# A gated feed-forward block after windowed attention: gate and up of two token chunks as a 2x2 block product with seven products

## The chip, the cores and the metric

One core of one Trainium2 chip. The metric is the time of one execution on the device in microseconds; three runs of the kernel before had a median of 698.26 us (697.82 to 700.38).

## What is computed

A pre-norm transformer block on x of 2048 tokens by 448: attention with 16 heads of 28 and a causal window of 256, then a gated feed-forward part of width 1792. All of it is in float32.

```python
h = x + attention(layernorm(x)) @ wo
y = layernorm(h)
g = y @ w_gate            # 448 x 1792
u = y @ w_up              # 448 x 1792
out = h + (gelu_tanh(g) * u) @ w_down   # 1792 x 448
```

## The kernel before, in words

**Numbers.** TensorE works in a float32 format with a shortened mantissa (fp32r). So every operand is split into a high part (`to_hi`, a copy on ScalarE) and a low part (`to_lo`, a subtraction on VectorE or GpSimd), and each product is the sum of three: high by high, low by high, high by low. A depth of 448 is three blocks of 128 rows and one of 64; the half blocks of two of the three products are laid on each other, so that a product of depth 448 takes 11 matmuls (`TERMS`, `NP`) where 10.5 would do.

**Order.** A planner (`Lists`) receives every operation with engine, cost, key, tokens read and written, and PSUM bank, simulates the engines, refines the keys in `ROUNDS` rounds from `SEED`, and emits the instructions in that order. Each engine then runs its own queue in order and waits on semaphores. The numbers in `op(...)` are the planner's costs.

**Attention** fills the first part. The second layer norm (`layer_norms`, kind "ln2", and `turn`) writes a normalized tile of 128 tokens to DRAM transposed and reads it back into `xT`, split in high and low part; this goes on beside attention's end and the first products.

**Feed-forward.** `product(n, i, c, ...)` works on a tile of 128 of the 1792 hidden columns (i) and a chunk of 512 of the 2048 tokens (c): 14 tiles by 4 chunks, 56 products, in four groups of tiles (`GROUPS`). The first four (`PAIRED = 4`) are whole: 11 matmuls of 128 rows and 512 columns for gate and 11 for up. From the fifth on every matmul is cut into two of 64 rows that run at the same time in the two halves of the array, one for gate and one for up, then with the halves exchanged (`pair`, `phase`): 21 pairs instead of 22 whole matmuls. Then ScalarE makes the gelu (L1125), VectorE the product with up (L1127), ScalarE and VectorE the high and low part (L487, L490), and the down product follows: 12 pairs of 448 columns into four banks that add up over a group, and VectorE adds them to `hres` (L1158). Between phases ScalarE reads one element of a bank (`seen`, L1068), which orders the two halves. Weights: 14 records of 1472 columns are loaded by SyncE's queue into one of three raw buffers (`weight_load`) and split by ScalarE and VectorE (the first three with GpSimd, `weight_splits`) into seven places (`RECS`).

All matmuls pass through the helper `mul` (L484), all high parts through L487, all low parts through L490: these lines are told apart by their tiles.

Of the kernel before, what the change touches and what calls it, by code (L numbers as in the profile page):

```python
# [18 lines left out]
NG = 4  # L19
# [6 lines left out]
GROUPS = [3, 4, 4, 3]  # L26
REC = 2944
NB = NG * CS
# [12 lines left out]
LEAD = 110  # L41
# [3 lines left out]
SWAP = -60  # L45
# [3 lines left out]
AHEAD = 7  # L49
BEHIND = 5  # L50
# [3 lines left out]
PAIRED = 4  # L54
MOVED = 0
SPANS = {"pp", "proj", "raw", "xT", "h", "rqf", "rkf", "vm", "rec0", "rec1", "rec2"}
# [13 lines left out]
ROUNDS = 220  # L70
SEED = 33
# [295 lines left out]
def block_kernel(ctx: ExitStack, tc, x, wqk_in, wv_in, wo_in, ffn_in, out):  # L367
# [16 lines left out]
    xT = pool.tile([128, 7, S], F32R, name="xT")  # L384
    rq_m = pool.tile([128, 4096], F32R, name="rq")
    rk_m = pool.tile([128, 6144], F32R, name="rk")
# [7 lines left out]
    last_hi = pool.tile([128, 128], F32R, name="lasthi")  # L394
    mhl = [pool.tile([128, 96], F32R, name=f"mhl{i}") for i in range(3)]
# [10 lines left out]
    back = pool.tile([128, 40], F32, name="back")  # L406

# [12 lines left out]
    ohl = lp.tile([128, 2, 2, 512], F32R, name="ohl")  # L420
    rec = []

    def open_rec():
        fst.close()
        p = ctx.enter_context(tc.tile_pool(name="fp", bufs=1))
        rec.extend(p.tile([128, REC], F32R, name=f"rec{i}") for i in range(2))
        rec.append(p.tile([128, S], F32R, name="xh"))


    rq = [rq_m[:, 2048 * u:2048 * u + 2048].rearrange("p (j t) -> p j t", j=4) for u in range(2)]  # L430
# [141 lines left out]
    def turn(t, key):  # L572
        c = slice(t * 128, (t + 1) * 128)
        d = xn_d[t]
        xb, at = (v_m[:, REC:REC + D], span("vm", REC, D)) if t > 7 and t % 2 else (xn[1], ("xn", 1))
        op("dve", 0.56, 0.65, key, lambda: nc.vector.transpose(xb, xn[0]), [("xn", 0)], [at], port=True)
        for a in range(4):
            dst = d.rearrange("(b i) t -> i b t", i=32)[:, :, 32 * a:32 * a + 32]
            src = xb[32 * a:32 * a + 32].rearrange("i (b t) -> i b t", t=32)
            dma(key, 150, lambda dst=dst, src=src: nc.sync.dma_start(dst, src), [at], [("xnd", t, a)])  # L580
        put = [("xnd", t, a) for a in range(4)]
# [13 lines left out]
        op("act", 0.7, 0.82, key + 0.2, hi, [("xt3", t)], [XT(t), "lasthi"])  # L595
        op("dve", 0.75, 0.82, key + 0.2, lo, [XT(t), "lasthi"], [XT(t)], port=True)
# [357 lines left out]
    def flat(m, name, o):  # L954
# [5 lines left out]
    RECS = [(lambda o=o, m=m, name=name: flat(m, name, o), flat(m, name, o)[1], need) for m, name, o, need in (  # L960
        (proj_m, "proj", 0, None), (proj_m, "proj", REC, None), (rq_m, "rqf", 0, "ringfree"),
        (rk_m, "rkf", 0, "ringfree"), (rk_m, "rkf", REC, "ringfree"))] + \
# [47 lines left out]
    def feed_forward():  # L1010
# [32 lines left out]
        for m in range(PAIRED, n):  # L1043
            for ph in phase[m]:
                order += [ph, todo.pop(0)]
# [270 lines left out]
```

## Time and profile before

| | us |
|---|---|
| median of three runs | 698.26 |
| profiled execution | 698.08 |
| its span, first to last instruction | 696.4 |
| TensorE busy | 687.8 |
| VectorE busy | 396.9 |
| ScalarE busy | 362.4 |
| GpSimd busy | 158.7 |

A busy time is the sum of what the engine's records cover. Matmuls overlap in the pipe, so the length of one record (0.376 us for a matmul of 512 columns) is longer than the distance to the next; what a matmul costs is read from the distance between starts. The same holds for VectorE. "PEld" is the load of weights, which runs beside the matmuls.

### The profile page before, as it was taken

What the parts mean: (1) busy time and instruction counts of PE and PEld (TensorE: products, weight loads), DVE (VectorE), ACT (ScalarE), POOL (GpSimd) and SP (SyncE); (2) the same over time, 40 slices, a digit from 0 to 9 for tenths busy, and PEclk for the clock granted to TensorE, in tenths of its full rate; (3) what the DMA queues carried; (4) which work ended last, traced back from release to release, by engine and by line L of the source; (5) the groups of instructions that cost most, each with busy time, mean ns of one, the idle gap of its engine ahead of it and who ended that gap; (6) DMA issues with size and microseconds to landing.
All of it is one profiled execution on the core that took longest, in us unless ns stands there. A gap on an engine that the chain in (4) does not pass through costs nothing.

```text
span 696.4 us, 15402 instructions
## 1 busy us (share of the span) xinstructions
PE 687.8 (99%) x5897; PEld 604.7 (87%) x5897; DVE 396.9 (57%) x1057; ACT 362.4 (52%) x930; POOL 158.7 (23%) x253
## 2 busy tenths in 40 slices
PE   8999999999999999999999999999999999999997
PEld 8998888888888887778899999999999999999996
DVE  7987877876687978877764232245232244333224
ACT  7658767776767888896653222234222234222221
POOL 5604434344454653753100000000000000000000
PEclk9999999999999999999999999999999999999999
DMA  8888647475556688524663000012100000001012
GB/s 297 262 282 243 210 150 229 141 213 164 176 168 197 160 247 226 157 55 95 146 188 131 1 2 2 1 44 88 45 1 2 1 1 2 1 1 55 10 45 106
DMA packets 83138, 79.12 MB, mean 114 GB/s; under 512 B 34104, under 2 KB 72952, under 8 KB 83064
## 3 DMA queue, kind: packets, MB, share of 16 engines
q1 hardware_dynamic: 83064, 78.14, 37.4%
q8 instruction: 46, 0.75, 0.4%
q14 instruction: 28, 0.23, 0.1%
HBM read 48.23 MB, written 29.36 MB: 111 GB/s over the span
## 4 chain that ended last, share of the span: by engine, by line
PE 91%; ACT 3%; DVE 3%; issue 1%; POOL 1%; DMA 0%; DVEq 0%; ACTq 0%
PE bank L484 85%; PE bank L894 5%; PE bank L542 1%; ACT pp L864 1%; ACT xn L537 1%; ACT xT L487 1%; DVE bnst L519 1%; ACT rq L487 0%; DVE xT L490 0%; DVE mt L792 0%; DVE hres L941 0%; POOL bnve L511 0%; PE bank L819 0%; DMA hres<-in_x_dram 0%; ACT proj L487 0%
## 5 line engine op out<-in xcount | busy, mean ns | idle before, releaser
L484 PE MATMUL bank<-xT,proj 64*128 64x512 f32 (+1 forms) x907 | 177.1, 381 | 0.0
L792 DVE CUSTOM_DVE_ANT_0 mt<-bank,mt 128x384 bf16<-128x384 f32 (+2 forms) x256 | 129.4, 528 | 34.4 <-PE bank L484 29.4
L864 ACT ACTIVATE pp<-bank 128x384 f32<-128x384 f32 (+2 forms) x352 | 124.1, 390 | 44.8 <-PE bank L484 39.1
L484 PEld LDWEIGHTS bank<-xT,proj 64*128 64x128 f32 (+1 forms) x907 | 118.6, 188 | 11.9 <-issue 0.8
L1127 DVE TENSOR_TENSOR mt<-bank,mt 128x512 f32<-128x512 f32 x54 | 37.2, 688 | 129.3 <-ACT mt L1125 129.3
L875 POOL TENSOR_SCALAR_AFFINE_SELECT pp<-pp 128x512 f32<-128x512 f32 x120 | 75.6, 643 | 114.3 <-ACT pp L864 109.6
L484 PE MATMUL bank<-rq,rk 104*128 104x384 f32 (+2 forms) x352 | 97.3, 297 | 0.8 <-ACT pp L864 0.4
L1125 ACT ACTIVATE mt<-bank 128x512 f32<-128x512 f32 x54 | 32.2, 596 | 108.5 <-PE bank L484 108.5
L484 PE MATMUL bank<-rk,rq 84*128 84x384 f32 (+2 forms) x256 | 81.5, 333 | 0.6 <-DVE proj L490 0.5
L1068 ACT ACTIVATE word<-bank 1x1 f32<-1x1 f32 x162 | 25.4, 157 | 106.7 <-PE bank L484 106.4
L484 PEld LDWEIGHTS bank<-rq,rk 104*128 104x128 f32 x352 | 65.5, 189 | 14.3 <-ACT pp L864 4.0
L484 PE MATMUL bank<-xT,rk 64*128 64x512 f32 x656 | 77.7, 376 | 0.0
L484 PE MATMUL bank<-xT,rec 64*128 64x512 f32 x656 | 77.7, 376 | 0.0
L484 PEld LDWEIGHTS bank<-xT,rec 64*128 64x128 f32 x656 | 63.6, 186 | 7.2
L484 PEld LDWEIGHTS bank<-xT,rk 64*128 64x128 f32 x656 | 63.6, 186 | 7.2
L1158 DVE TENSOR_TENSOR hres<-bank,hres 128x448 f32<-128x448 f32 x64 | 35.5, 617 | 59.5 <-ACT mt L1125 33.8
L484 PE MATMUL bank<-proj,xT 128*128 128x224 f32 x352 | 58.0, 275 | 0.0
L490 DVE TENSOR_TENSOR proj<-mt,proj 128x512 fp32r<-128x512 f32 x54 | 37.3, 692 | 35.7 <-ACT proj L487 30.7
L484 PEld LDWEIGHTS bank<-rk,rq 84*128 84x128 f32 x256 | 48.1, 190 | 8.3 <-issue 2.9
L484 PEld LDWEIGHTS bank<-proj,xT 128*128 128x128 f32 x352 | 51.8, 191 | 0.9
L484 PE MATMUL bank<-wos,ohl 128*128 128x448 f32 x192 | 51.4, 365 | 0.2 <-DVE mx L792 0.2
L487 ACT ACTIVATE proj<-mt 128x512 fp32r<-128x512 f32 x54 | 34.0, 629 | 31.0 <-DVE mt L1127 30.0
(109 smaller groups left out, 967.6 us busy)
## 6 DMA issues: line engine op xcount, KB each, us to landing
rk<-k SPq DMA_DIRECT2D x44, 336.0 KB
rq<-q SPq DMA_DIRECT2D x32, 336.0 KB
q<-proj SPq DMA_DIRECT2D x15, 448.0 KB
raw<-in_ffn_dram SPq DMA_DIRECT2D x7, 736.0 KB
v<-in_ffn_dram SPq DMA_DIRECT2D x7, 736.0 KB
k<-proj SPq DMA_DIRECT2D x11, 448.0 KB
hres<-in_x_dram SPq DMA_DIRECT2D x16, 224.0 KB
out_dram<-hres SPq DMA_DIRECT2D x16, 224.0 KB
```

Of the source, the lines that this page charges most:

```text
L484: nc.tensor.matmul(o.rearrange("p (t h) -> p t h", h=2), w, mixed(m), **how)
L487: nc.scalar.activation(dst, src, AF.Copy)
L490: (eng or nc.vector).tensor_sub(dst, src, f(hi))
L519: op("dve", 0.65, 0.63, key(t), lambda t=t: nc.vector.bn_stats(bnst[t % 2], hres[:, t, :]), [HR(t)], [("bnst", t % 2)])
L792: nc.vector.tensor_tensor_reduce(plain(junk[s % 2][:, o:384]), unmixed(bank[b.k][:, o:384]), plain(mask[:, o:384]), 1.0, -BIG, OP.add, OP. ...
L864: nc.scalar.activation(plain(pp[:, j, o * 128:o * 128 + n]), unmixed(bank[b.k][:, 0:n]), AF.Exp, scale=SCALE)
L875: nc.gpsimd.affine_select(a, a, pattern=[[0, 4], [-cm, 128]], compare_op=op_, fill=0.0, base=0, channel_multiplier=cm)
L894: nc.tensor.matmul(bank[b.k][32 * j:32 * j + DH + 1, lo * 128:(hi + 1) * 128], v[:, 4 * c - 2 + m, g % 2, j, :], pp[:, j, at[m] * 128:(at[ ...
L1068: op("act", 0.08, 0.17, key, lambda: nc.scalar.activation(word[0:1, 0:1], bank[b.k][0:1, 0:1], AF.Copy), (), (), b)
L1125: op("act", 0.485 + table, 0.608 + table, key + NP, lambda: nc.scalar.activation(plain(g2), src(0), AF.Gelu_apprx_tanh), held[0], G2, bs[0 ...
L1127: op("dve", 0.605, 0.702, key + 2 * NP, lambda: nc.vector.tensor_tensor(plain(g2), src(1), plain(g2), op=OP.mult), [*G2, *held[1]], G2, bs ...
L1158: op("dve", 0.533, 0.626, key + 2 * NP + 3 * q + 3, lambda t=t, b=down[q]: nc.vector.tensor_tensor(plain(hres[:, t, :]), unmixed(bank[b.k] ...
```

## The change

Two chunks of tokens (X1, X2) and the two weights (gate, up) of a tile of hidden columns make a 2x2 block product. The depth of 448 is taken as 192 + 192 + 64. On the two depths of 192 the four results come from seven products of sums and differences of the blocks instead of eight, in the order P1, P6, P7, P5, P2, P4, P3; the remaining 64 rows are stacked below four of them (P2, P3, P4, P7). Each of the seven keeps its three parts (high by high, low by high, high by low): 5 matmuls of 128 rows for P1, P5, P6 and 6 for the others, 39 for a **unit** of two products, where two paired products had 42 pairs.

What goes with it:
- `combine(p, i, key)`: for a pair of chunks p and 128 of its tokens in each (i from 0 to 3) it loads the normalized tiles from DRAM (8 DMAs), forms the sums and differences on VectorE (6 instructions), the high parts on ScalarE (4) and the low parts on VectorE (10). The high parts of pair 0 lie in the half of `xT` of the chunks 2 and 3 and the other way round.
- `record(i, j, key, gate)`: a weight tile is loaded into one raw buffer, GpSimd forms the differences (7 instructions), ScalarE the high parts, VectorE and GpSimd the low parts (5 and 4). There are 18 such loads in three slots, since some tiles are used for both pairs in a row.
- `unit(n, p, j)`: four banks take the seven products; ScalarE copies the first out (L1233), VectorE adds the others (L1229, five additions of 512 columns), then two gelus, two products (L1248), two high and two low parts.
- `down`: 12 matmuls of 128 rows for a product, no longer pairs; they add up over the two tiles of a segment (`SEGS`).
- The chunks 0 and 1 take the hidden tiles 0 to 3 (`FIRST`, `conv`) as 8 plain products of 22 matmuls while the X of pair 0 is made; 24 units do the rest. Layer norm tiles of the chunks 2 and 3 are no longer read back into `xT`.
- The buffers of q, k and the records become one tile `ring`, and the planner's seed and rounds are others.

```diff
-GROUPS = [3, 4, 4, 3]
...
+RS = 3584
+GC = 4
+FIRST = ((0, 0), (0, 1), (1, 0), (1, 1), (0, 2), (0, 3), (1, 2), (1, 3))
+SEGS = ((0, (4, 5)), (0, (6, 7)), (0, (8, 9)), (1, (8, 9)), (1, (6, 7)), (1, (4, 5)), (1, (0, 1)), (1, (10, 11)), (0, (10, 11)), (0, (12, 13)), (1, (12, 13)), (1, (2, 3)))
...
-PAIRED = 4
...
+ADDS = ("dve", "dve")
+LOP = ()
+SK = FFN + 128
+RK = 50
...
+    def combine(p, i, key):
...
+        def add(n, out, w, a, ar, b, br, key, op_=OP.subtract):
...
+                op("dve", 0.07 + n * 0.00104, 0.17 + n * 0.00104, key, lambda: nc.vector.tensor_tensor(out, a, b, op=op_),
+                   [*ar, *br, "mtfree"], w, port=True)
+
+        def sub(n, out, src, hi, r, w, key):
+            op("dve", 0.07 + n * 0.00104, 0.17 + n * 0.00104, key, lambda: to_lo(out(), src, hi), [*r, "fp"], w, port=True)
...
+        def parts_of(q, src, r, n, key):
+
+            hi = xT_m.rearrange("p (q h b t) -> p q h b t", q=7, h=2, b=2)[:, q:q + n, 1 - p, :, tok]
+            w = [[w for m in range(n) for w in XS(p, q + m, c, i)] for c in range(2)]
+            op("act", 0.07 + 256 * n * 0.0009, 0.17 + 256 * n * 0.0009, key, lambda: to_hi(hi, src),
+               [*r, "c1free" if p else "xfree"], w[0] + w[1])
+            k = LO_OF[q][0]
+            sub(128 * n, lambda: XL(p, k, n)[..., tok], src[:, :, 0], hi[:, :, 0], [*r, *w[0]],
+                [w for m in range(n) for w in XS(p, q + m, 2, i)], key)
...
+        add(256, E, e, two(1, 0, 4), at(1, 0, 4), two(1, 1, 4), at(1, 1, 5), key + 1, OP.add)
+        add(128, b(1, 0), at(1, 0), b(0, 0), at(0, 0), b(1, 0), at(1, 0), key + 1)
+        add(128, b(1, 2, LOW), at(1, 2), b(0, 2, LOW), at(0, 2), b(1, 4, LOW), at(1, 4), key + 1)
+        parts_of(0, both(0), at(0, 0, 1, 2, 3), 2, key + 1)
+        parts_of(6, E[:, None], e, 1, key + 1)
+        add(256, two(0, 0, 2), at(0, 0, 2), E, e, two(0, 0, 2), at(0, 0, 2), key + 2)
+        parts_of(4, both(1), at(1, 0, 1, 2, 3), 2, key + 2)
+        add(128, b(0, 1), at(0, 1), b(0, 1), at(0, 1), b(0, 0), at(0, 0), key + 2)
+        add(128, b(0, 3, LOW), at(0, 3), b(0, 3, LOW), at(0, 3), b(0, 2, LOW), at(0, 2), key + 2)
+        parts_of(2, both(0), at(0, 0, 1, 2, 3), 2, key + 2)
...
+    def record(i, j, key, gate):
...
+        take(256, E, e, blk[:, 4:9:4], rt(4, 8), blk[:, 0:3:2], rt(0, 2), key)
+        take(128, blk[:, 4], rt(4), blk[:, 5], rt(5), blk[:, 4], rt(4), key)
+        take(128, blk[LOW, 6], rt(6), blk[LOW, 6], rt(6), blk[LOW, 8], rt(8), key)
+        parts_of(0, g, rt(0, 1, 2, 3), 2, key)
+        take(256, blk[:, 0:3:2], rt(0, 2), blk[:, 5:10:4], rt(5, 9), E, e, key + 1)
...
+        parts_of(2, g, rt(0, 1, 2, 3), 2, key + 1)
+        parts_of(4, u, rt(4, 5, 6, 7), 2, key + 1)
+        parts_of(6, E[:, None], e, 1, key + 1)
...
+    def term(p, j, name, a):
...
+        part, wb, xb = ((0, 0, 0), (0, 1, 1), (1, 0, 0), (1, 1, 1), (0, 0, 2), (0, 1, 3))[a]
+        part = "lo" if part else "hi"
+        return R[part][:, w, wb], lambda: X(p, q)[:, xb] if xb < 2 else XL(p, LO_OF[q][xb - 2])[:, 0], XS(p, q, xb) + at(part, w, 1, (wb,))
...
+    PART1 = whole("P1", "P6", "P7", "P5")
+    PART2 = whole("P2", "P4", "P3")
...
+    def unit(n, p, j):
...
+        def play(steps, out, key):
...
+                start = i not in opened
+                opened.add(i)
+                out.append(op("pe", mm(512), 0.403, key + 0.2 * m, lambda w=w, x=x, i=i, start=start: mul(
+                    bank[bs[i].k], w, x(), start=start, stop=False, skip_group_check=True), r, (), bs[i]))
+
...
+        play(PART1, part1[n], key)
+        op("act", 0.49, 0.605, key + 2, lambda: nc.scalar.activation(plain(A), unmixed(bank[bs[0].k]), AF.Copy), (), ta, bs[0])
+        add(key + 3, A, ta, A, ta, 1)
+        add(key + 4, Bt, tb, A, ta, 2)
+        add(key + 4, Bt, tb, Bt, tb, 3)
+        yield
+        play(PART2, part2[n], key + 8)
+        add(key + 12, C, tc_, A, ta, 2)
+        add(key + 13, A, ta, A, ta, 3)
+        op("act", 0.485, 0.608, key + 12, lambda: nc.scalar.activation(
+            plain(G), unmixed(bank[bs[0].k]), AF.Gelu_apprx_tanh), (), tg, bs[0])
...
+            op("dve", 0.6, 0.7, key + 14 + side, lambda z=z, g=g: nc.vector.tensor_tensor(z, z, g, op=OP.mult), [*tz, *tgg],
+               tz, port=True)
+            op("act", 0.52, 0.635, key + 14 + side, lambda z=z, o=o: to_hi(o[:, 0:512], z), tz, [at[0]])
+            op("dve", 0.6, 0.7, key + 14 + side, lambda z=z, o=o: to_lo(o[:, 512:1024], z, o[:, 0:512]), [*tz, at[0]], [at[1]],
+               port=True)
+
+    slot = {}
...
+    def down(s, R, at, k, of, c, banks, key, closes, ends):
...
+    def conv(w, c, k):
...
-
-                todo = TERMS if ph else TERMS[:-1]
-                for a, (h, wb, xb) in enumerate(todo):
...
-                    phase[n][ph].append(pair(key + 11 * ph + a / NP, 512, 0.403, lambda side=side: side(0),
-                                             lambda side=side: side(1), need, bs))
-                if not ph:
...
-        PARTS = ((0, 0), (1, 0), (0, 1))
-        last = n == 4 * NF - 1
-        for ph in range(0 if last else 2):
...
-                        q = 2 * j + (x ^ ph ^ k % 2)
-                        return (down[q], gh(oh)[HALF[x], q, :], get()[0][2][wh][HALF[x]], not ph and k == 0 and a == 0,
...
+            next(half)
+            chain.extend(part1[n])
+            if n != 1 and n < len(units) - 1:
+                next_down()
+            at = len(chain)
+            if n:
+                next_down()
+            held = chain[at:]
+            del chain[at:]
+            if n == len(units) - 1:
+                m, name, o, _ = SLOTS[(loads - 3) % 3]
+                free += [(m, name, o), (m, name, o + 1024)]
+            for side in range(2):
+                slot[n, side] = free.pop(0)
+            next(half, None)
+            chain.extend(part2[n])
+            chain.extend(held)
+        while items:
```

Three places of the two programs' orders. First **TensorE** in the steady feed-forward part. Before, the end of one phase of a product and the start of its neighbour's down product: gate and up alternate between two banks (144 and 145), 64 rows each, and so do the down banks.

```order
L484 MATMUL bank_144<-xT,rq 128x512
L484 MATMUL bank_145<-xT,rq 128x512
L484 MATMUL bank_144<-xh,rq 128x512
L484 MATMUL bank_147<-proj 128x448
L484 MATMUL bank_146<-proj 128x448
```

Now the first half of a unit (P1, P6, P7 and P5 in the banks 138 to 141; `X_3862` holds low parts of X) and the start of a down product of 12:

```order
L489 MATMUL bank_138<-xT,ring 128x512 x4
L489 MATMUL bank_138<-X_3862,ring 128x512
L489 MATMUL bank_139<-xT,ring 128x512 x4
L489 MATMUL bank_139<-X_3862,ring 128x512
L489 MATMUL bank_140<-xT,ring 128x512 x4
L489 MATMUL bank_140<-X_3862,ring 128x512 x2
L489 MATMUL bank_141<-xT,ring 128x512 x4
L489 MATMUL bank_141<-X_3862,ring 128x512
L489 MATMUL bank_142<-ring,proj 128x448 x3
```

Every matmul now has 128 rows, and a bank takes its matmuls in a row.

Second **VectorE**. Before, a product late in the feed-forward part: the product with up, its low part, and the additions of a finished chunk.

```order
L1127 TENSOR_TENSOR mt<-bank_143,mt 128x512
L490 TENSOR_TENSOR proj<-mt,proj 128x512
L1158 TENSOR_TENSOR hres<-bank_146,hres 128x448
L1158 TENSOR_TENSOR hres<-bank_147,hres 128x448
L1158 TENSOR_TENSOR hres<-bank_148,hres 128x448
L1158 TENSOR_TENSOR hres<-bank_149,hres 128x448
L1127 TENSOR_TENSOR mt<-bank_145,mt 128x512
```

Now the end of unit 5 and the first addition of unit 6, the first unit on the second pair of chunks (`X_3862`, `xT`, `ring<-mt,xT` and `proj<-v,xT` are parts of its X):

```order
L495 TENSOR_TENSOR ring<-mt,ring 128x448
L495 TENSOR_TENSOR X_3862<-v,xT 128x128
L1248 TENSOR_TENSOR v<-v 128x512
L495 TENSOR_TENSOR xT<-v,xT 64x128
L495 TENSOR_TENSOR X_3862<-v,xT 128x2x128
L495 TENSOR_TENSOR proj<-v,xT 128x2x128
L495 TENSOR_TENSOR xT<-mt,xT 64x128
L495 TENSOR_TENSOR ring<-mt,xT 128x128
L495 TENSOR_TENSOR proj<-v,proj 128x512
L1248 TENSOR_TENSOR v<-v 128x512
L495 TENSOR_TENSOR proj<-raw,proj 128x2x128
L1229 TENSOR_TENSOR v<-v,bank_139 128x512
```

The last pieces of X for the second pair stand between the unit's own products, up to the unit that uses them.

Third **GpSimd**. Before, its last work is this, at the start of the feed-forward part:

```order
L490 TENSOR_TENSOR rq<-raw,rq 128x448
L510 TENSOR_SCALAR bnve<-bnmv 128x2
L511 TENSOR_TENSOR bnve<-bnve,nhalf 128x2
L515 TENSOR_TENSOR bnve<-bnmv,bnve 128x2
L516 TENSOR_SCALAR bnve<-bnve 128x2
```

Now there is a record of differences and low parts for each load up to the end, such as:

```order
L1155 TENSOR_TENSOR v<-raw 128x256
L495 TENSOR_TENSOR ring<-raw,ring 128x2x128
L1155 TENSOR_TENSOR raw<-raw,v 128x2x128
L1155 TENSOR_TENSOR raw<-raw 64x128 x2
L1155 TENSOR_TENSOR raw<-raw 128x128 x2
L1155 TENSOR_TENSOR raw<-raw 64x128
L495 TENSOR_TENSOR ring<-raw,ring 128x2x128
L495 TENSOR_TENSOR ring<-v,ring 128x128
L495 TENSOR_TENSOR ring<-raw,ring 128x2x128
```

All of these have two inputs in SBUF.

440 lines of the change are left out of this document (298 added, 142 removed).

## The prediction

> **What bounds the kernel now.** I read the page first: the shares of the engines and the forty slices.
>
> ```profile
> PE 687.8 (99%) x5897; PEld 604.7 (87%) x5897; DVE 396.9 (57%) x1057; ACT 362.4 (52%) x930; POOL 158.7 (23%) x253
> ...
> PE   8999999999999999999999999999999999999997
> ...
> DVE  7987877876687978877764232245232244333224
> ...
> POOL 5604434344454653753100000000000000000000
> PEclk9999999999999999999999999999999999999999
> ```
>
> TensorE is busy 99% of the span at full clock. VectorE is the second engine in the first half only, and GpSimd does nothing in the second half. The stretches (span start to attention's end, the changeover, the feed-forward part) put numbers to this; each row gives PE, PEld, DVE, ACT and POOL busy.
>
> ```profile
> 20.00:300.00 280.00, 278.49 (x2088) 233.36 (x2086) 224.03 (x753) 210.85 (x530) 129.32 (x186) 1.00 0.67 200
> 300.00:333.00 33.00, 32.31 (x233) 26.03 (x234) 23.78 (x49) 25.07 (x63) 15.69 (x26) 1.00 0.35 76
> 333.00:691.00 358.00, 358.00 (x3467) 328.18 (x3466) 131.60 (x218) 110.59 (x315) 1.48 (x4) 1.00 0.13 39
> ```
>
> TensorE idles 1.5 us in attention, 0.7 us in the changeover, and not at all in 358 us of feed-forward, where VectorE is busy 131.6 us (37%). The chain that ended last says the same: one unbroken run of matmuls.
>
> ```profile
> 332.53 358.43 PE bank L484 x3467
> 691.06 0.71 DVE hres L1158 x2
> ```
>
> So here a matmul removed is its full pitch gained, as long as the other engines keep up, and they have 60% of their time free before the change.
>
> **What the change removes on TensorE.** The order of the two programs gives the counts. Half-height matmuls run two at a time; I call a pair or one full-height matmul a slot. Before, gate and up take 4 whole products of 22 slots and 52 paired ones of 21: 88 + 1092 = 1180. After: 8 plain products of 22 and 24 units of 39 (each two products): 176 + 936 = 1112. That is **68 slots of 512 columns fewer**. The down products take 672 slots of 448 columns in both, and attention's matmuls have the same counts. What a slot costs, full-height and paired, stands in the timeline of TensorE (start, length, tile, count):
>
> ```profile
> 317.81 4.05 PE L484 MATMUL bank<-xT,rq 128*128 128x512 f32 x18
> 321.70 1.49 PE L484 MATMUL bank<-wos,ohl 128*128 128x448 f32 x7
> ...
> 335.36 1.30 PE L484 MATMUL bank<-rq,proj 64*128 64x448 f32 x12
> 336.50 2.53 PE L484 MATMUL bank<-xT,proj 64*128 64x512 f32 x21
> 338.66 0.38 PE L484 MATMUL bank<-xh,proj 64*128 64x512 f32 x1
> 338.87 1.30 PE L484 MATMUL bank<-rq,proj 64*128 64x448 f32 x12
> ```
>
> 18 full-height matmuls take 321.70 - 317.81 = 3.89 us, 0.216 us each; 11 pairs take 338.87 - 336.50 = 2.37 us, 0.215 us each. A pair costs what a full-height matmul costs, so 68 x 0.216 = **14.7 us** go. Six pairs of 448 columns take 336.50 - 335.36 = 1.14 us, 0.19 us each; full-height ones stay at that or below (7 in 1.49 us with the last one's tail), so the down part changes by nothing. The 162 one-element reads on ScalarE between phases go too, off the path.
>
> **What it adds, and where that lies.** In a unit, VectorE now has five additions from PSUM, two products and two subtractions of 512 columns where two products before had four instructions; each fresh weight record gives it five subtractions and GpSimd eleven; each of eight groups of 128 tokens gives VectorE 16 short instructions (the differences and low parts of X). Their prices are the distances from start to start in VectorE's timeline:
>
> ```profile
> 326.95 1.28 DVE L490 TENSOR_TENSOR proj<-v,proj 128x512 fp32r<-128x512 f32 x2
> 328.15 0.62 DVE L941 TENSOR_TENSOR hres<-bank,hres 128x448 f32<-128x448 f32 x1
> ...
> 360.30 2.22 DVE L1158 TENSOR_TENSOR hres<-bank,hres 128x448 f32<-128x448 f32 x4 [1.07 <-PE bank L484]
> 362.44 0.68 DVE L1127 TENSOR_TENSOR mt<-bank,mt 128x512 f32<-128x512 f32 x1
> ```
>
> 512 columns: 1.20 / 2 = 0.60 us; 448 columns: 2.14 / 4 = 0.535 us; so 1.02 ns a column, and by that slope 0.34 us for 256 columns and 0.21 us for 128. That is the cheap end. The dear end is an instruction that does not overlap its neighbour:
>
> ```profile
> 254.20 0.56 DVE L490 TENSOR_TENSOR xT<-xT 128x384 fp32r<-128x384 f32 x1
> 254.79 0.29 DVE L490 TENSOR_TENSOR xT<-xT,lasthi 64x128 fp32r<-64x128 f32 x1
> 255.11 0.56 DVE L792 CUSTOM_DVE_ANT_0 mt<-bank,mt 128x384 bf16<-128x384 f32 x1
> ```
>
> Here 128 columns take 0.32 us and 384 take 0.59 us, so 256 take about 0.455 us. [...]
>
> From unit 6 on this is covered: the order puts 14 to 19 VectorE instructions in a unit, at most about 10 us at the dear end, and TensorE's unit is 39 x 0.216 + 24 x 0.19 = 13.0 us. If that cover went, each further microsecond would be paid once a unit.
>
> The place that decides is earlier: **from attention's last projection to the start of unit 6**. In that stretch TensorE has 110 + 234 = 344 slots of 512 columns and 204 of 448: 74.3 + 38.8 = 113.1 us. VectorE has, by the order, 66 instructions of 512 columns (39.6 us), 39 of 448 (20.9), 66 of 256, 86 of 128, and 14 transposes and statistics of the second layer norm. The rows for those 14, and behind them one for ScalarE and one for SyncE's queue:
>
> ```profile
> L519 DVE BATCH_NORM_STATS2 bnst<-hres 128x6 f32<-128x448 f32 x32 | 19.5, 613 | 1.9 <-DMA hres<-in_x_dram 1.7
> L576 DVE STREAM_TRANSPOSE xn<-xn 128x448 f32<-128x448 f32 x12 | 7.6, 637 | 1.5 <-ACT xn L537 1.2 <-ACT pp L864 0.4
> ...
> L487 ACT ACTIVATE proj<-mt 128x512 fp32r<-128x512 f32 x54 | 34.0, 629 | 31.0 <-DVE mt L1127 30.0 <-PE bank L484 0.9
> ...
> 334.82 1.88 SPq L580 DMA_DIRECT2D xn<-xn  x4
> ```
>
> Ten of them go at about 0.55 us (0.08 under the lengths in the groups, as 0.60 is under 0.69 at 512 columns), four are short: 5.8 us. Cheap: 39.6 + 20.9 + 22.4 + 18.1 + 5.8 = 106.8 us. Dear: 39.6 + 20.9 + 30.0 + 27.5 + 5.8 = 123.8 us. The middle, 115.3 us, is already 2.2 us over TensorE, with the order fixed on both engines, so what VectorE is late by stands ahead of unit 0 or of units 2 to 6 as TensorE's idle time. [...]
>
> ScalarE gets five instructions a unit and five a record, ten of at most 0.63 us in 13.0 us: covered. On SyncE's queue the stretch has about 110 issues (64 loads for X, the stores of the layer norm, the records' loads) of 1.88 / 4 = 0.47 us, 52 us of 113: covered as a sum; but the records now share one raw buffer, so a record's load waits for GpSimd to have read the one before, and X's loads stand behind it. That wait costs nothing while a record is ready a unit early, and at its worst a unit of 13.0 us once; I take nothing, since the three record slots let the load run ahead.
>
> Then GpSimd. Its prices, from the groups and the timeline:
>
> ```profile
> L490 POOL TENSOR_TENSOR ohl<-oT,ohl 128x512 fp32r<-128x512 f32 x15 | 19.2, 1279 | 4.6 <-ACT ohl L487 2.7 <-PE bank L484 1.9
> L490 POOL TENSOR_TENSOR wos<-raw,wos 128x448 fp32r<-128x448 f32 x4 | 4.6, 1143 | 2.4 <-ACT wos L487 2.3
> ...
> 281.38 2.52 POOL L490 TENSOR_TENSOR proj<-raw,proj 128x512 fp32r<-128x512 f32 x2
> 283.85 0.64 POOL L875 TENSOR_SCALAR_AFFINE_SELECT pp<-pp 128x512 f32<-128x512 f32 x1
> ```
>
> 136 ns for 64 columns is 2.1 ns a column, and a pitch of 2.47 / 2 = 1.235 us at 512; so 0.69 us for 256 and 0.42 us for 128. A record is five of the first and six of the second: 6.0 us, 108 us for all 18, six of them (36 us) inside that stretch, with four groups of layer norm instructions (about 1.4 us each) 42 us of 113, or 37%. As load it fits under 13.0 us a unit. But the two engines get in each other's way:
>
> ```profile
> 299.87 0.64 POOL L875 TENSOR_SCALAR_AFFINE_SELECT pp<-pp 128x512 f32<-128x512 f32 x1 [2.57 <-ACT pp L864]
> ...
> 299.92 0.99 DVE L490 TENSOR_TENSOR xT<-xT 128x384 fp32r<-128x384 f32 x1
> ...
> 303.76 0.52 DVE L490 TENSOR_TENSOR xT<-xT 128x384 fp32r<-128x384 f32 x1
> ...
> L490 DVE TENSOR_TENSOR xT<-xT 128x384 fp32r<-128x384 f32 x16 | 9.4, 587 | 2.1 <-ACT xT L487 2.0
> ```
>
> A subtraction with both inputs in SBUF took 0.99 us beside a GpSimd instruction and 0.52 us without. On the mean it took 0.587 us; alone an instruction of 384 columns takes the 0.56 us of the row at 254.20, so about 0.03 us was lost each time with GpSimd busy 129.3 of 280 us (46%). Of the 271 instructions in the stretch 189 have two such inputs: 189 x 0.03 x 37/46 = 4.6 us. [...]
>
> VectorE's lateness is then 2.2 + 4.6 = 6.8 us. The last pieces of X for unit 6 are used some 2 us into it, so about **5 us** reach TensorE. The attention part is drawn anew by the planner (another seed) with the same instructions: I keep its 1.5 us of idle, plus or minus 1.5. The end is alike: a last down product, four additions, the store.
>
> **The sum**, against the profiled execution: 698.1 (696.4 of span and 1.7 around it) - 14.7 + 5 = **688.4 us**. Its 698.1 stands 0.2 under the median of 698.26.
>
> **The rivals.**
> *The cover holds throughout*: VectorE goes at the cheap end, 106.8 us under 113.1, and the planner keeps the two-input instructions clear of GpSimd. For it: the loss above is 0.03 us on the mean; and between 333 and 691 us TensorE waited for nobody. Against it: nothing in this trace shows VectorE full for 100 us; in attention it is busy 80%. Time: 698.1 - 14.7 = 683.4.
> [...]
> [...]
> *A full-height matmul is dearer than a pair after all*: 936 slots; at 0.232 us instead of 0.216 the gain is gone. The 18 in a row at 0.216 us speak against it.
>
> **How the numbers follow.** A measurement of this kernel can tell about 0.5% (3.5 us) from no change. Forecast (3 to 9 us lost, 686 to 693): 0.50. Cover holds (682 to 686): 0.23. Dear end (693 to 700): 0.17. Lock sets the pace: 0.08. Dearer matmuls or another mishap: 0.02. Under 694.8 us lie the first two and a little of the third: 0.76. Within 0.5%: 0.14. Slower: 0.10. The range from 682.5 to 699 leaves out the last two cases and the edges.
>
> **What would show it.** The pitch of the units' matmuls should be 0.216 us and a unit from the sixth on 13.0 us, with TensorE full. TensorE's idle time should lie in two places, ahead of unit 0 and in units 2 to 6, released by VectorE's low parts of X or its additions (L1229), and add up to about 5 us. VectorE should be over 90% busy in those 113 us. I am wrong if idle time recurs in every unit (GpSimd's records late, or banks freed late), if the units' matmuls go at another pitch, or if the attention part moves by more than 1.5 us.

## The result, and the profile after

| | before | after |
|---|---|---|
| median, us | 698.51 (20 runs, 697.82 to 700.38) | 699.18 (20 runs, 697.12 to 702.72) |
| ratio | | 1.0008, 95% interval 0.9997 to 1.0019 |
| profiled execution, us | 698.08 | 702.72 |
| its span, us | 696.4 | 701.0 |

No change that can be measured, where 688.4 was forecast. The profiled execution of after is its slowest run, 3.5 us over its median; 1.7 of its 702.72 us lie around the span. The head of its page:

```profile
PE 680.3 (97%) x4077; PEld 591.9 (84%) x4077; DVE 565.4 (81%) x1397; ACT 392.6 (56%) x860; POOL 285.7 (41%) x451
...
PE   8999999999999999899999999899999999999997
...
DVE  7987887766597978787898999987888786876765
...
POOL 5603544434446644754313456235455450620200
PEclk9999999999999999999998999999999999999999
```

TensorE is busy 7.5 us less than before, while the span is 4.6 us longer: its matmuls went and idle time came. VectorE is at eight or nine tenths from the 21st slice to the 27th (350 to 473 us), and the clock strip has an 8 where it had only nines. By stretch (PE, PEld, DVE, ACT and POOL busy, clock): the three of the prediction, then attention's last projection up to unit 6, the units after it, and one unit alone.

```profile
20.00:300.00 280.00, 274.98 (x2063) 227.19 (x2061) 222.10 (x737) 207.60 (x518) 129.48 (x186) 1.00 0.66 200
300.00:333.00 33.00, 32.33 (x215) 25.83 (x214) 26.51 (x58) 26.12 (x63) 15.47 (x23) 1.00 0.33 80
333.00:691.00 358.00, 349.58 (x1668) 317.39 (x1667) 297.44 (x563) 143.47 (x257) 128.94 (x206) 0.99 0.22 66
328.40:456.80 128.40, 119.98 (x550) 106.13 (x549) 121.09 (x269) 62.19 (x113) 48.62 (x80) 0.96 0.36 98
456.80:650.00 193.20, 193.20 (x941) 177.44 (x940) 152.07 (x257) 72.45 (x130) 76.49 (x123) 1.00 0.18 57
...
521.55:534.51 12.96, 12.96 (x65) 11.91 (x65) 11.24 (x19) 5.94 (x12) 6.39 (x11) 1.00 0.27 78
```

The units from the sixth on are as forecast: 193.2 us without a gap, 12.96 us a unit. What was gained there went in two places. One is attention: 5.0 us of idle in the first row, where there were 1.5. With the changeover it comes to 6.0 us, by TensorE's timelines around the last projection, first after, then before:

```profile
324.69 3.86 PE L489 MATMUL bank<-wos,ohl 128*128 128x448 f32 x19 [0.53 <-DVE ohl L495]
328.39 2.69 PE L489 MATMUL bank<-proj 128*128 128x448 f32 x12
```

```profile
326.91 0.35 PE L484 MATMUL bank<-wos,ohl 128*128 128x448 f32 x1
327.19 2.27 PE L484 MATMUL bank<-proj 64*128 64x448 f32 x18
```

After, attention ends 1.2 us later although one plain product of 22 matmuls fewer (4.75 us) lies ahead of its end. The other place is the fourth row, **the stretch** of the prediction: 128.4 us for TensorE's 113.1 us of work, 15.3 us lost. Its waits there:

```profile
PE bank L489 <- DVE hres L1278: 3.0, 1, 3.0
PE bank L489 <- DVE v L1229: 2.7, 2, 2.1
PE bank L489 <- POOL ring L495: 1.5, 1, 1.5
PE bank L489 <- DVE ring L495: 0.9, 2, 0.7
```

These waits make up 8.1 of the 8.4 us of idle in the row (128.4 - 119.98). Another 4.7 us are half clock: in the two windows below TensorE is busy for 5.92 + 3.40 = 9.3 us at half its speed. The last 2.2 us stand in no wait; a matmul's record (0.376 us) is longer than the distance to the next (0.216), so each record hides some of the gap behind it. TensorE's timeline around the longest wait, and the windows of half clock:

```profile
363.88 2.43 PE L489 MATMUL bank<-ring,proj 128*128 128x448 f32 x12
369.28 4.82 PE L489 MATMUL bank<-ring,proj 128*128 128x448 f32 x12 [2.97 <-DVE hres L1278]
373.89 1.69 PE L489 MATMUL bank<-xT,proj 128*128 128x512 f32 x4
```

```profile
368.40:375.20 6.80, 5.92 (x16) 5.18 (x17) 5.67 (x13) 1.68 (x3) 2.10 (x4) 0.50 0.39 131
...
450.30:453.70 3.40, 3.40 (x9) 2.68 (x9) 2.70 (x9) 1.12 (x3) 0.00 (x0) 0.50 0.00 0
```

The 12 matmuls behind the wait take 373.89 - 369.28 = 4.61 us, 0.38 each, where the 12 ahead of it went at 0.19. Together: 6.0 + 15.3 - 14.7 = 6.6 us slower, against 4.6 measured between the two profiles; 2.0 us of this sum I can't place (0.55 us that the kernel before idles in its own 132.8 us from 327.2 to 460 are part of it). VectorE's queue shows why the first wait is there:

```profile
364.31 0.69 DVE L495 TENSOR_TENSOR proj<-mt,proj 128x512 fp32r<-128x512 f32 x1
364.92 0.42 DVE L684 TENSOR_TENSOR v<-mt,v 128x256 f32<-128x256 f32 x1
...
367.59 0.29 DVE L495 TENSOR_TENSOR xT<-v,xT 64x128 fp32r<-64x128 f32 x1
367.91 0.69 DVE L1323 TENSOR_TENSOR mt<-bank,mt 128x512 f32<-128x512 f32 x1
368.52 2.21 DVE L1278 TENSOR_TENSOR hres<-bank,hres 128x448 f32<-128x448 f32 x4
```

The next down product needs the banks that L1278 empties. TensorE had filled them at 366.2; the additions stand behind a row of short instructions on X and the weights, without a gap, and start at 368.5.

### The profile page after: what moved, and what is told of

Same layout as the page of the kernel before. It is cut to its first block, busy times and chain, and to the rows that moved or that the text cites. A ratio compares the mean times of both kernels' runs of the same rounds, so it can differ in the third digit from the quotient of the medians.

```text
span 701.0 us, 12311 instructions
## 1 busy us (share of the span) xinstructions
PE 680.3 (97%) x4077; PEld 591.9 (84%) x4077; DVE 565.4 (81%) x1397; ACT 392.6 (56%) x860; POOL 285.7 (41%) x451
## 4 chain that ended last, share of the span: by engine, by line
PE 74%; DVE 12%; ACT 5%; DMA 4%; issue 2%; POOL 2%; SPq 1%; DVEq 0%; ACTq 0%; POOLq 0%
PE bank L489 68%; PE bank L1017 5%; ACT pp L987 2%; DVE proj L495 2%; DMA hres<-in_x_dram 1%; DVE xT L495 1%; DVE hres L1278 1%; DVE v L1229 1%; DVE X L495 1%; DVE bnst L524 1%; DMA ring<-q 1%; ACT ring L492 1%; DMA xn<-xn 1%; ACT xT L492 1%; DVE v L684 1%
## 5 line engine op out<-in xcount | busy, mean ns | idle before, releaser
L489 PE MATMUL bank<-xT,proj 128*128 128x512 f32 x620 | 178.4, 386 | 0.8 <-DVE xT L495 0.5
L489 PE MATMUL bank<-ring 84*128 84x384 f32 (+6 forms) x618 | 154.9, 316 | 3.1 <-ACT pp L987 1.7
L489 PE MATMUL bank<-xT,ring 128*128 128x512 f32 x536 | 137.2, 383 | 5.4 <-DVE v L1229 2.7
L489 PE MATMUL bank<-ring,proj 128*128 128x448 f32 (+1 forms) x628 | 129.3, 357 | 3.0 <-DVE hres L1278 3.0
L489 PEld LDWEIGHTS bank<-ring 104*128 104x128 f32 (+2 forms) x618 | 107.7, 189 | 26.1 <-ACT pp L987 5.5
L489 PEld LDWEIGHTS bank<-ring,proj 128*128 128x128 f32 x628 | 120.2, 192 | 6.7 <-issue 3.3
L489 PEld LDWEIGHTS bank<-xT,proj 128*128 128x128 f32 x620 | 113.8, 191 | 12.5 <-DVE xT L495 0.9
L489 PEld LDWEIGHTS bank<-xT,ring 128*128 128x128 f32 x536 | 101.7, 191 | 20.8 <-DVE v L1229 3.5
L1229 DVE TENSOR_TENSOR v<-v,bank 128x512 f32<-128x512 f32 x120 | 82.0, 684 | 44.4 <-PE bank L489 41.6
L1278 DVE TENSOR_TENSOR hres<-bank,hres 128x448 f32<-128x448 f32 x112 | 63.9, 616 | 2.6 <-PE bank L489 2.6
L489 PE MATMUL bank<-X,ring 128*128 128x512 f32 x146 | 48.6, 382 | 0.0
```

What stands on the lines that cost most here:

```text
L489: nc.tensor.matmul(o.rearrange("p (t h) -> p t h", h=2), w, mixed(m), **how)
L1229: op("dve", 0.605, 0.702, key, lambda: nc.vector.tensor_tensor(plain(out), plain(a), unmixed(bank[bs[i].k]), op=OP.add), ar, w, bs[i])
L1278: op("dve", 0.533, 0.626, key + 3 * q + 3, lambda t=t, b=banks[q]: nc.vector.tensor_tensor(plain(hres[:, t, :]), unmixed(bank[b.k][:, 0:D] ...
```

## The experiments

Three theories of where the 15.4 us between 683.8 (698.5 - 14.7) and 699.2 went. **Theory 1**: VectorE's work in the stretch, slowed beside GpSimd, is what TensorE waits for. **Theory 2**: the weight records come late from GpSimd. **Theory 3**: the planner's new drawing (seed and rounds) lost time in attention. In the kernels "in its own order" the planner's final keys are written into the program, so that every engine's order is that of the changed kernel but for the edit.

**Less work for VectorE and GpSimd (e1, e2, e6).** e1 leaves VectorE's differences of X out, e2 six of GpSimd's seven differences of each record, e6 both.

```diff
@@ e1, combine @@
-lambda: nc.vector.tensor_tensor(out, a, b, op=op_),
+(lambda: None) if op_ == OP.subtract else lambda: nc.vector.tensor_tensor(out, a, b, op=op_),
@@ e2, record @@
-lambda: nc.gpsimd.tensor_tensor(out, a, b, op=OP.subtract),
+lambda: nc.gpsimd.tensor_tensor(out, a, b, op=OP.subtract) if out is E else None,
```

> The changed kernel in its own order on every engine, with the 40 subtractions of VectorE that form the differences of X left out (five for each of eight groups of 128 tokens; the sums are still made, so X has wrong blocks and the output is not the reference's). Theory 1 (VectorE's amount of work in the stretch from attention's last projection to unit 6 is what TensorE waits for): these 40 took 16.9 us there by their means (8 of 256 columns at 0.48, 32 of 128 at 0.41 us), VectorE falls from 121 to about 105 us, under TensorE's 113, and 11 to 15 of the 15.3 us lost there come back: 684 to 688 us, 0.980 to 0.985 of the kernel before. Theory 2 (the weights come late from GpSimd): only some meetings with GpSimd go, 3 to 5 us: 694 to 696 us, 0.994 to 0.997. The attention part stays as it is in both.

> The changed kernel in its own order, with six of GpSimd's seven differences of each weight record left out (108 instructions; wrong weights, so the output is not the reference's). In the stretch up to unit 6 about 20 of GpSimd's 48.6 us go. Theory 1 with the two engines in each other's way: VectorE's two-input instructions lose 14 us in all beside GpSimd there, some 40% of it comes back: 5 to 6 us, 693 to 694 us, 0.992. Theory 2 (records late): the waits of TensorE and VectorE for GpSimd go in full, 2 to 4 us directly, and what they delay, so 690 or less. Rival (GpSimd costs nothing): within 1 us of the changed kernel, 698 to 700 us, 1.000.

> The changed kernel in its own order with both left out that e1 and e2 left out apart: VectorE's 40 differences of X and 108 of GpSimd's of the weights (wrong blocks, so the output is not the reference's). If what is lost is VectorE's work and its slower pace beside GpSimd, the two gains of 4.3 and 4.6 us add up, to 690 us, 0.987; the floor is 688 to 689, since the attention part (6 us in the profile) stays lost. Rival (single places of the fixed order that wait whatever the load): no more than 6 us, 693 us or more.

Measured: e1 694.79 us, 0.9939 (0.9924 to 0.9954); e2 694.27, 0.9937 (0.9924 to 0.995); e6 690.71, 0.9888 (0.9871 to 0.9904). The stretch in e1 and TensorE's longest wait there (total, times, longest), the stretch in e2, and stretch and wait in e6:

```profile
327.50:449.40 121.90, 117.52 (x551) 103.99 (x550) 111.95 (x229) 61.08 (x113) 46.97 (x80) 0.99 0.39 104
```

```profile
PE bank L489 <- DVE v L1229: 2.9, 3, 2.1
```

```profile
327.50:448.30 120.80, 115.00 (x550) 103.04 (x549) 115.51 (x267) 61.83 (x112) 28.55 (x42) 1.00 0.39 104
```

```profile
327.40:446.40 119.00, 115.75 (x551) 104.59 (x550) 107.43 (x229) 61.14 (x113) 27.90 (x42) 0.99 0.40 106
```

```profile
PE bank L489 <- DVE v L1229: 3.3, 2, 1.9
```

e2 came out as theory 1 said, within 1 us: with 20 us less of GpSimd in the stretch, VectorE needs 115.5 us in place of 121.1 for the same instructions. The groups that share the time with GpSimd, first of after, then of e2 (mean ns behind the comma):

```profile
L495 DVE TENSOR_TENSOR X<-v,xT 128x256 fp32r<-128x256 f32 x27 | 12.6, 478 | 1.7 <-POOL bnve L520 1.1 <-ACT xT L492 0.4
...
L684 DVE TENSOR_TENSOR v<-v 128x128 f32<-128x128 f32 x16 | 6.6, 413 | 0.1
```

```profile
L495 DVE TENSOR_TENSOR X<-v,xT 128x256 fp32r<-128x256 f32 x27 | 11.7, 441 | 1.6 <-POOL bnve L520 1.0 <-ACT xT L492 0.6
...
L684 DVE TENSOR_TENSOR v<-v 128x128 f32<-128x128 f32 x16 | 5.5, 341 | 0.1
```

e1 missed theory 1: 4.4 us back, not 11 to 15, and its 694.79 lies in the range written down for theory 2 (694 to 696). Against theory 2 speak e2, for which it had 690 or less, and the waits above, of which only 1.5 us are for GpSimd. The 40 instructions were worth 9 us of VectorE's time, not 16.9 (records overlap, as the one of 0.69 us at 364.31 does with the next, which starts 0.61 us behind it, so a sum of means counts too much), and VectorE at 112.0 us is now under TensorE's 113.1; still the stretch takes 121.9. In e6, at 107.4, it takes 119.0. The wait ahead of P4 in unit 5, 2.1 us in after, is 2.1 in e1 and 1.9 in e6, and the clock of the stretch is 0.99 in both: in e1 the 12 matmuls of 512 columns behind the wait take 4.28 us (442.71 to 446.99) where 12 x 0.216 = 2.59, so 1.7 us go. So **the sums alone do not set the loss**: theory 1 holds in part. That the rest comes of where work stands in the queues is argued from such waits, not shown by e1 and e6. The gains of e1 and e2 nearly add up (4.4 and 4.9 apart, 8.5 together against the changed kernel).

**One place of the queue (e10).** The additions that TensorE waited for (L1278) and the product ahead of them go ahead of the ten short instructions.

```diff
@@ VectorE's order at the end of the plain products @@
+TENSOR_TENSOR mt<-bank_139,mt 128x512
+TENSOR_TENSOR hres<-bank_142,hres 128x448
+TENSOR_TENSOR hres<-bank_143,hres 128x448
+TENSOR_TENSOR hres<-bank_144,hres 128x448
+TENSOR_TENSOR hres<-bank_145,hres 128x448
...
-TENSOR_TENSOR mt<-bank_139,mt 128x512
-TENSOR_TENSOR hres<-bank_142,hres 128x448
-TENSOR_TENSOR hres<-bank_143,hres 128x448
-TENSOR_TENSOR hres<-bank_144,hres 128x448
-TENSOR_TENSOR hres<-bank_145,hres 128x448
```

> The changed kernel with one place of VectorE's order edited: the last plain product's product with up and the four additions to hres behind it (2.8 us of work, which empty the banks for the next down product) now stand ahead of the ten short instructions on X and the weights that were ahead of them; all else is the same. Theory 1 (VectorE's amount of work): the 3.0 us of wait ahead of the down product go, and unit 0 waits for X instead, 698.5 to 700 us, 1.000. Rival (the place in the queue alone): the wait goes, and with it the half clock behind it in the runs that have it, 695 to 696.5 us, 0.996.

Measured: 702.76 us, 1.0051 (1.0035 to 1.0066): slower than either theory said. TensorE's timeline:

```profile
366.60 2.51 PE L493 MATMUL bank<-ring,proj 128*128 128x448 f32 x12 [0.79 <-DVE hres L1282]
...
370.99 0.92 PE L493 MATMUL bank<-xT,proj 128*128 128x512 f32 x3 [0.59 <-DVE xT L499]
...
377.26 1.65 PE L493 MATMUL bank<-xT,proj 128*128 128x512 f32 x3 [3.16 <-DVE xT L499]
```

The wait of 3.0 us ahead of the down product shrank to 0.8 and stands again in unit 0, 3.2 us, where the last of X's parts is late. That is theory 1's mechanism, a wait that moves and does not go; half clock follows it there too (the three matmuls of 512 columns behind it take 1.44 us, 0.48 each). With VectorE full, this edit of its queue only chose who waits.

**The clock (e7, e9).** Matmuls with zero weights use up two waits.

```diff
@@ both (in e7 start and stop are False) @@
+    def filler(b, count, m):
+        for _ in range(count):
+            mul(b[0:32, 0:m.shape[-1]], zero, m, start=m.shape[-1] == D, stop=m.shape[-1] == D, skip_group_check=True)
@@ e7, down and unit @@
+            fill = 16 if not res and key == FFN + 16 * 7 + 24 else 0
+                fill = 10 if (n, name, a) == (5, "P4", 0) else 0
@@ e9, down and unit @@
+            fill = 14 if not res and key == FFN + 16 * 6 + 24 else 0
+                fill = 8 if (n, name, a) == (5, "P4", 0) else 0
```

> The changed kernel in its own order with 26 matmuls added whose weights are zero (32 columns; they add nothing to an open bank): 16 of 448 columns (3.0 us) ahead of the last plain product's down product, where TensorE waited 3.0 us, and 10 of 512 columns (2.2 us) ahead of P4 in unit 5, where it waited 2.1. They use up the wait, so TensorE is not idle. If the half clock comes of that idleness, it is gone from the clock's record; the profiled execution had lost 5.1 us to it, the middle execution less: 696 to 698 us, and the slowest executions (702) are gone. Rival (the half clock has another cause, or VectorE is what is late anyhow): 699 us within 1, with or without a half clock.

> As e7 with the first group at its right place: 14 zero-weight matmuls of 448 columns (2.7 us) into an unused bank ahead of the down product at which TensorE waited 3.0 us, and 8 of 512 columns (1.7 us) ahead of P4 in unit 5. If the half clock comes of TensorE's idle time there, every run has a clock of 0.998 or more and the median is that of the changed kernel's runs with 0.999, 697 to 698 us (0.998), with none over 700. Rival (another cause): the mean clock stays at 0.997 over the runs, 699 us.

e7 measured 702.52 us, 1.0061 (1.0044 to 1.0078). My first group was at a wrong place: the eighth product's down matmuls run inside unit 0, and there the fillers only cost their 3.0 us. e9 has them at the wait: 698.83 us, 1.0000 (0.9988 to 1.0011).

```profile
365.45 2.81 PE L489 MATMUL bank<-ring,pad 128*32 128x448 f32 x14
368.58 2.51 PE L489 MATMUL bank<-ring,proj 128*128 128x448 f32 x12 [0.32 <-DVE hres L1284]
```

```profile
368.40:375.20 6.80, 6.18 (x29) 5.36 (x29) 6.74 (x14) 2.52 (x5) 3.27 (x5) 1.00 0.29 106
...
327.40:452.80 125.40, 119.98 (x573) 105.30 (x572) 120.95 (x268) 62.49 (x112) 49.37 (x80) 1.00 0.37 100
```

The same window that had 0.50 now has 1.00, and 10 of e9's 12 runs have a mean clock of 0.999 or more, where 5 of the changed kernel's 20 have. So the half clock at these two places does come of TensorE's idle time. But the median hardly moved, 0.35 us with intervals that overlap: at full clock the stretch still takes 125.4 us, with VectorE's work at 121.0. The changed kernel's own five runs at 0.999 say the same: their median is 698.56 us. The half clock makes the slowest runs (the four over 700 us have 0.992 to 0.995); it is not where the forecast gain went.

**The drawing (e8, e11, e3).** e8 is the kernel before with the planner's ROUNDS and SEED of after, e11 the changed kernel with those of before, e3 the changed kernel with attention's beginning in the order of the kernel before.

```diff
@@ e8, on the kernel before; e11 is the reverse on the changed kernel @@
-ROUNDS = 220
-SEED = 33
+ROUNDS = 230
+SEED = 3
```

> The kernel before, nothing changed but the planner's seed and rounds, which are those of the changed kernel (ROUNDS 230, SEED 3). Theory 3 (another drawing of the same work costs several us by itself): 701 to 704 us, 1.004 to 1.008. Rival (the drawing is worth nothing, what attention lost comes of the new work beside it): 698 to 699.5 us, within 0.1%.

> The changed kernel with nothing changed but the planner's seed and rounds, which are those of the kernel before (ROUNDS 220, SEED 33). Theory 3 (the drawing is worth several us either way): 701 to 705 us, or 694 to 697, in any case over 2 us from the changed kernel's 699.2. Rival (the loss belongs to the work and not to the drawing): 698 to 700.5 us.

> The changed kernel whole, but attention in the order of the kernel before (the first 1749 matmuls on TensorE in the same order); the rest planned again around it. Theory 3 (the order of attention lost 6 us): those come back, 693 us, 0.993, if VectorE's lateness ahead of unit 0 does not grow. Rival (VectorE is what is late, and an earlier end of attention only lengthens the wait ahead of unit 0): 698 to 700 us, 1.000.

Measured: e8 702.47 us, 1.005 (1.0035 to 1.0064); e11 699.76, 1.0013 (1.0002 to 1.0024); e3 697.03, 0.998 (0.9963 to 0.9998). The kernel before loses 3.8 us to the new seed alone (its own median beside e8 is 698.68), as theory 3 expected. Most of it is one place of its timeline, a short wait with half clock behind it (0.50 from 281.8 to 288.6 us with TensorE busy for 6.48 us, 3.2 lost):

```profile
281.41 0.67 PE L484 MATMUL bank<-rq,rk 104*128 104x128 f32 x3 [1.10 <-ACT pp L864]
282.39 0.80 PE L484 MATMUL bank<-rq,rk 104*128 104x128 f32 x2 [0.32 <-ACT pp L864]
282.98 4.90 PE L484 MATMUL bank<-xT,proj 128*128 128x512 f32 x11
```

For the changed kernel the other seed is worth nothing in the time (e11; theory 3 missed), but the parts moved against each other. The stretch takes 6.8 us less than in after, with its half clock, and 3.8 less than in e9; this drawing leaves 261 of VectorE's instructions in it, 117.0 us, where after has 269 and 121.1. Attention ends 2.3 us later, at 330.7, with a clock of 0.99 from 20 to 300 us where after has 1.00, and behind the stretch 1.3 us more go (245.5 us in place of 244.2):

```profile
330.70:452.30 121.60, 116.27 (x551) 102.79 (x551) 116.96 (x261) 61.19 (x111) 49.99 (x80) 1.00 0.37 101
```

So the drawing also decides how much of VectorE's work falls into the stretch. e3 got back about 2 of the 6 us: with the old order TensorE idles as little as in the kernel before up to 280 us, but at the changeover it waits 2.4 us for a high part of the last output projection, which the rest, planned around it, no longer covers:

```profile
322.12 4.61 PE L489 MATMUL bank<-wos,ohl 128*128 128x448 f32 x21 [2.39 <-ACT ohl L492]
```

**When the second pair is first used, and at what price the order is planned (e4, e12, e5).** All three keep attention's beginning of the kernel before, as e3. e4 uses the second pair from unit 8, e5 from unit 10. In e5 and e12 the planner reckons 0.05 us more for each short instruction on VectorE; e12 keeps the segments of the changed kernel.

```diff
@@ e5 (e4 goes to pair 1 after four segments) @@
-SEGS = ((0, (4, 5)), (0, (6, 7)), (0, (8, 9)), (1, (8, 9)), (1, (6, 7)), (1, (4, 5)), (1, (0, 1)), (1, (10, 11)), (0, (10, 11)), (0, (12, 13)), (1, (12, 13)), (1, (2, 3)))
+SEGS = ((0, (4, 5)), (0, (6, 7)), (0, (8, 9)), (0, (10, 11)), (0, (12, 13)), (1, (12, 13)), (1, (10, 11)), (1, (8, 9)), (1, (6, 7)), (1, (4, 5)), (1, (0, 1)), (1, (2, 3)))
@@ e5 and e12, combine and record @@
-op("dve", 0.07 + n * 0.00104, 0.17 + n * 0.00104, key,
+op("dve", 0.12 + n * 0.00104, 0.22 + n * 0.00104, key,
```

> As e3, and the second pair of chunks is first used by unit 8 in place of unit 6 (one more segment on the first pair ahead of it, 20 weight records in place of 18), so that VectorE has 26 us longer for its X. Theory 1: of the 9.5 us lost in units 0 to 5 some 2 remain: with the attention part back 686 us, 0.982; without it 692. Rival (what is late is the first pair's X, the layer norm or SyncE's queue, all ahead of unit 0): as e3, within 1 us.

> As e5 (attention's beginning in the order of the kernel before, the planner reckoning 0.05 us more for each short instruction of VectorE, planned again), but with the changed kernel's own segments: the second pair is used from unit 6, 18 weight records. Theory 1 (VectorE's amount of work in the stretch): no order gets the stretch under VectorE's work, some 120 us against TensorE's 113, and little is gained on e3: 694 to 697 us, 0.995. Rival (what was wrong was the order, drawn from prices that were too low for the short instructions): near e5, 688 to 690.5 us, 0.986.

> As e4, but the second pair is first used by unit 10 (22 weight records), and the planner reckons 0.05 us more for each short instruction of VectorE. In e4's profile 2.0 us were still lost ahead of unit 0, 1.6 in the units 0 to 7, 2.2 at the first use of the second pair in unit 8, and 1.7 by a half clock at attention's end. Theory 1 (VectorE's work per unit sets it): with two more units to spread it over, most of the 3.8 us in the units go and the rest stays: 688 to 690 us, 0.986. Rival (the four further records put back on VectorE and GpSimd what the spreading took off): 692 to 694 us, 0.992.

Measured: e4 692.44 us, 0.9912 (0.9895 to 0.9928); e12 692.95, 0.9913 (0.9898 to 0.9929); e5 **688.14, 0.985 (0.9833 to 0.9867)**, which beats both kernels. The same matmuls, last projection to unit 6, in e4, in e12 and then in e5:

```profile
328.10:444.00 115.90, 114.06 (x550) 103.46 (x550) 112.58 (x241) 56.65 (x102) 52.87 (x85) 1.00 0.35 96
```

```profile
323.90:445.10 121.20, 116.79 (x550) 102.53 (x550) 117.65 (x262) 62.52 (x112) 50.34 (x80) 1.00 0.39 106
```

```profile
323.90:440.40 116.50, 114.61 (x550) 103.07 (x549) 109.17 (x235) 58.75 (x107) 51.79 (x85) 1.00 0.37 101
440.40:492.30 51.90, 51.90 (x255) 47.70 (x254) 50.55 (x107) 26.74 (x49) 25.19 (x39) 1.00 0.32 87
```

e4 came to what theory 1 expected without attention's part back (692). At the old price its stretch takes 115.9 us where e3's takes 122.6; what it loses lies elsewhere, in an end of attention 1.7 us later than e3's and in 1.8 us of waits at the second pair's first use, in unit 8.

e12 lies between the two theories. Order and price bring 4.1 us over e3 with VectorE's work in the stretch all but unchanged (117.7 us after 118.5). Most of it is the changeover: the product behind the last projection starts at 324.1 us in place of 326.6 (the rows of e12 and e5 begin 0.2 us ahead of it). The stretch itself goes only from 122.6 to 121.2 us, 8.1 over TensorE's 113.1, and with 117.7 us of VectorE's work left in it, it cannot take less than that. That floor goes when the second pair moves: in e5 VectorE has 109.2 us in the stretch and catches up in the units 6 to 9, 50.6 of 51.9 us busy, with TensorE full beside it. TensorE loses 3.4 us in the stretch, and behind the four units it is busy for 147.6 of the 147.7 us up to 640, so the four more records cost it nothing there.

The later pair shortens the stretch at both prices, by 6.7 us (e3 to e4) and 4.7 (e12 to e5). Each of these kernels is one drawing, though, and a drawing can be worth as much: 3.8 us of time in e8, 6.8 us of the stretch in e11. No run repeats e4, e12 or e5 with another seed, so the shares below are those of these drawings.

## Why the prediction was wrong

*Matmul price and count: right.* The 68 slots are gone at the price forecast: 12.96 us a unit (13.0 forecast), TensorE full from unit 6 on, nothing recurring in the units; e5 has most of the gain in its time. The rival "a full-height matmul is dearer" falls. VectorE's 19 instructions of a unit take 11.2 us, where at most 10 were reckoned; they are still covered.

*VectorE's work in the stretch: right, nearly.* Forecast 115.3 + 4.6 = 119.9 us, measured 121.1 (after) and 121.0 (e9). GpSimd's part of it is larger than forecast: 38 of its 80 instructions left out of the stretch (e2) saved VectorE 5.6 us, where I had 4.6 for all of them; so some of the work itself must have gone at less than the middle price. No run shows a reason to take the middle price, nor the lock of the case "lock sets the pace" (0.08). What the runs showed in their place: 128 columns (L684) took 413 ns on the mean with 48.6 us of GpSimd's work in the stretch (after) and 341 ns with 28.6 us of it (e2), and all of VectorE's work there came to 121.1 us. The time, 699.18 us, lies in the range given for the dear end (693 to 700), but by luck: the dear end is 123.8 + 4.6 = 128.4 us of VectorE's work, and no loss in attention is part of it.

*The step that failed: "The last pieces of X for unit 6 are used some 2 us into it, so about 5 us reach TensorE."* I took the difference of two sums, 6.8 us, less a cover of 2, as if VectorE never waited and its lateness were paid once. Measured in its place: 128.4 - 113.1 = 15.3 us in the profiled run, 12.3 in e9 at full clock (125.4), 4.4 of it fillers in place of waits. VectorE itself stood idle for 7.3 us (128.4 - 121.1) in the stretch with its order fixed; 4.1 of them are its additions waiting for TensorE's matmuls (busy and mean, then the idle time ahead of them and what ended it):

```profile
L1229 DVE TENSOR_TENSOR v<-v,bank 128x512 f32<-128x512 f32 x30 | 20.3, 678 | 4.4 <-PE bank L489 4.1
```

So each engine waits for the other in turn, and the difference of the sums has only one of the two. And where VectorE is not late by the sum it can be late at a place: in e1 with 112.0 us of work the stretch lost 8.8 us, 1.7 of them by the clock. Four drawings with a clock of 1.00 in the stretch give the size: it takes VectorE's work in it and 3.5 to 4.6 us on top (e12 121.2 for 117.7, e3 122.6 for 118.5, e9 125.4 for 121.0, e11 121.6 for 117.0). So the sum of the work was nearly right; in place of 2 us of cover there were some 4 us of waits. With the second pair later, where VectorE's work is under TensorE's, the stretch loses 2.8 us (e4) and 3.4 (e5).

*The second: "I keep its 1.5 us of idle, plus or minus 1.5."* The attention part lost 3.5 us up to 300 us, and 6.0 to the last projection. e8 shows that the drawing alone can cost as much (3.8 us on the kernel before), so a new seed is a term of its own; one drawing each way does not give its range. e3 suggests that part of the 6 us belongs to the new work at the changeover: the old order of attention brought its end from 328.4 only to 326.6, and dearer prices as well (e12) to 324.1, where 22 matmuls fewer would give 327.2 - 4.75 = 322.4.

*Where idle time was to be looked for*: ahead of unit 0 and in the units 2 to 6, released by VectorE's low parts or L1229: places right, releasers half. The longest wait is for L1278, 1.5 us are GpSimd's, and 4.7 us are half clock, which the prediction did not have at all. The profiled run is the slowest; in the middle run the half clock costs some 0.6 us (699.18 against the 698.56 of the runs at 0.999).

In medians: e5's 688.14 is 10.4 us under before, of the 14.7; after's 699.18 gave back 15.4. Of the 11.0 us between after and e5, e3 has 2.2, the order at better prices 4.1 (e12), the later second pair 4.8. In the profiles e3 has both an earlier end of attention (1.8 us) and a shorter stretch (122.6 against e9's 125.4), so its 2.2 us are not attention's alone.

## What to carry to other kernels

Where two engines are nearly equally full over a stretch, do not take the difference of their sums as the loss: with in-order queues each one's local waits add, and the stretch took 3.5 to 4.6 us more than the fuller engine's work at full clock, and 7.3 in the profiled run of after with its half clock. Moving five instructions up only moved the wait. What helped was to ask when the new data is first needed and to spread the work that makes it over a stretch with room (here one or two segments later); an order planned with prices nearer the measured ones also came out better, in one drawing. A change that redraws an order by search carries the scatter of the drawing, 3.8 us in the one case tried on the kernel before, and belongs beside a redrawn kernel before.

## What the runs showed of the hardware

TensorE's clock fell to half at short waits: in after at one of 2.97 us (0.50 from 368.4 to 375.2 us) and at one of 2.07 (0.50 from 450.3 to 453.7), and in e8 behind one of 1.10 us followed by 0.32 (0.50 from 281.8 to 288.6; the 11 matmuls of 512 columns went at 0.43 us each). It did not fall in e2 behind waits of 2.0 and 1.8 us (1.00 from 365 to 372 and from 440 to 452), and e3 had one of 2.6 in a stretch with a clock of 1.00. Matmuls with 32 columns of zero weights, in place of the wait, kept the clock at 1.00 from 368.4 to 375.2 in e9's profile.

In after TensorE was busy for 1.31 of the 3.40 us ahead of the first fall (365.0 to 368.4) and for 1.35 of the 3.42 ahead of the second (446.88 to 450.3). In e2 it was busy for 5.04 of the 7.00 us around the wait of 2.0, and the clock stayed. How much idle time sets off a fall, or where it has to lie, no run tests. In e12 the clock from 20 to 300 us is 0.99 with no wait up to 330 us over 0.4 us, and in e11 it is 0.99 there with none up to 470 us over 1.1; what set it off in these two is open.
